# A ConvNeXt block on one core: convolution two tiles ahead and layernorm one tile ahead, both spread over the octets of the MLP

## The chip, the cores and the metric

The kernel runs on one core of a Trainium2 chip. A core has a matrix engine (PE, with its weight loads shown apart as PEld), a vector engine (DVE), a scalar engine (ACT), a general engine (POOL), and SyncE (SP), which here only issues transfers. The matrix engine writes into PSUM, a small memory of its own; everything else lies in SBUF. Each engine works through its own queue in order, and waits where a semaphore has not come yet.

The metric is the device time of one execution in microseconds, lower is better. A profile is one execution taken by the hardware profiler: it gives the start and the length of each instruction, and what its engine waited for.

## The reference

```python
def reference(x, dw, w1, b1, w2, b2, gamma):        # x: 1 x 512 x 512 x 96, bf16
    xp = jnp.pad(x, ((0,0),(pad,pad),(pad,pad),(0,0)))
    for i in range(3):
        for j in range(3):
            out = out + xp[:, i:i+H, j:j+W, :] * dw[i, j][None, None, None, :]
    h = _layernorm(out, axis=-1)
    h = jnp.einsum('bhwc,ce->bhwe', h, w1) + b1      # 96 -> 384
    h = _gelu(h)
    h = jnp.einsum('bhwe,ec->bhwc', h, w2) + b2      # 384 -> 96
    return x + gamma[None, None, None, :] * h
```

A depthwise 3x3 convolution, a layernorm over the 96 channels, an MLP with gelu, a scale by gamma, and a residual.

## The kernel before

**Tiles.** The image is cut into 20 tiles: four strips of 128 rows, each cut into five blocks of 102 or 103 columns. A tile goes through three stages.

1. *Convolution* (`conv_steps`, L156). `load_xw` (L141, transfer on L151, on SP) brings the tile's pixels into `xw`, with columns of the image on the partitions. For each channel three matmuls (L168), one for each vertical offset, multiply `xw` by a band matrix `brev` that holds the three horizontal taps. Four channels, 12 matmuls, make a "quad" in one PSUM tile `ps_conv` (two buffers). A quad is then evacuated into `zt`, three of four by DVE (L173) and every fourth by ACT (L175). A tile has 24 quads.
2. *Layernorm* (`ln_steps`, L182). For each of the 102 or 103 columns DVE takes statistics of the 96 channels (L189). The columns are worked in four parts; after the statistics of a part, POOL computes the reciprocal deviation (six small operations, then a power, L200) and multiplies `zt` by it in place (L201). The mean is not subtracted: it is folded into the weights at the start.
3. *MLP* (`mlp_octet`, L214), eight columns at a time, called an octet; a tile has 13, the last one shorter. PE transposes eight columns into `pst` (L218, one PSUM buffer), they are copied to `y` (by ACT, L221, or by DVE, L223), six matmuls make `h` (L235, two buffers), three gelus on ACT make `gt` (L239, four buffers), and for each column four matmuls make `po` (L251 and L255, one PSUM buffer for four columns). DVE adds the residual `xh` to four columns at a time (L259) and SP stores the octet (L262). The residual `xh` of an octet is loaded on SP (L211) two octets ahead, in three buffers.

**Order.** At the start two tiles are loaded, and tile 0 gets its convolution and its layernorm. Then one loop runs over all octets of all tiles (L312). While tile `ti` goes through its octets, the generator `chain` (L298) gives the work of tile `ti + 1`: in the first half of the octets (`CONV_FRAC` 0.5, six octets) its 24 quads, four to an octet; in the second half its layernorm steps. In that second half `y` is copied by ACT, else by DVE. The load of tile `ti + 2` is issued at the start of tile `ti`. `xw` has two buffers and `zt` two.

The program text sets which work is before which where both are ready. What each engine's queue holds in the end is laid out when the program is built; the trace shows it.

**Start.** The band matrix is made from a table `r_dram` by eight transfers (L100), four issued by SP and four by POOL, each 36 x 128 runs of 127 elements.

The parts that the change touches:

```python
    xw_pool = ctx.enter_context(tc.tile_pool(name="xw", bufs=2))
    zt_pool = ctx.enter_context(tc.tile_pool(name="zt", bufs=2))
    ...
            if c4 % EVAC_MOD != EVAC_MOD - 1:
                nc.vector.tensor_copy(out=zt[:, :n, 4 * c4:4 * c4 + 4], in_=ps[:, :, :n].rearrange("p s q -> p q s"))
            else:
                nc.scalar.copy(out=zt[:, :n, 4 * c4:4 * c4 + 4], in_=ps[:, :, :n].rearrange("p s q -> p q s"))
```

Of the kernel before, what the change touches and what calls it, by code (L numbers as in the profile page):

```python
# [8 lines left out]
BF16 = mybir.dt.bfloat16  # L9
F32 = mybir.dt.float32  # L10
# [3 lines left out]
P = 128  # L14
NMAX = 126
# [3 lines left out]
def _w_blocks(W):  # L19
    blocks = []  # L20
    w0 = 0
    nblk = -(-W // NMAX)
    sizes = [W // nblk + (1 if i < W % nblk else 0) for i in range(nblk)]
    for n in sizes:
        lo = max(0, w0 - 1)
        hi = min(W, w0 + n + 1)
        need = hi - lo
        kload = min(P, -(-need // 16) * 16)
        c_base = lo
        extra = kload - need  # L30
# [12 lines left out]
def kernel(  # L43
# [11 lines left out]
    nc = tc.nc  # L55
    B_, H, W, C = x.shape
# [4 lines left out]
    CA = C + 1  # L61
    NM = 3 * C
    NB = NMAX + 1
    RL = 256

    const = ctx.enter_context(tc.tile_pool(name="const", bufs=1))
    dram = ctx.enter_context(tc.tile_pool(name="dram", bufs=1, space=bass.MemoryType.DRAM))

# [3 lines left out]
        out=ident[:], in_=ident[:], pattern=[[-1, P]], compare_op=ALU.not_equal,  # L72
        fill=1.0, base=0, channel_multiplier=1,
    )

    mhalf = const.tile([P, NMAX], F32, name="mhalf")
    nc.gpsimd.memset(mhalf[:], -0.5)
    sel0 = const.tile([P, P], BF16, name="sel0")
    nc.vector.memset(sel0[:], 0.0)
# [12 lines left out]
    brev = const.tile([P, NM, NB], BF16, name="brev")  # L92
    NCH = 8
    mper = NM // NCH
    for ch in range(NCH):
        m0 = ch * mper
        src = bass.AP(tensor=r_dram.tensor, offset=r_dram.offset + m0 * RL,
                      ap=[[1, P], [RL, mper], [1, NB]])
        with nc.allow_non_contiguous_dma("hankel band expansion"):
            (nc.sync if ch % 2 == 0 else nc.gpsimd).dma_start(out=brev[:, m0:m0 + mper, :], in_=src)  # L100

    w1s = const.tile([C, E], BF16, name="w1s")
    nc.sync.dma_start(out=w1s[:], in_=w1)
# [21 lines left out]
                                       op0=ALU.mult, op1=ALU.add)  # L125

    xw_pool = ctx.enter_context(tc.tile_pool(name="xw", bufs=2))
    zt_pool = ctx.enter_context(tc.tile_pool(name="zt", bufs=2))
    st_pool = ctx.enter_context(tc.tile_pool(name="st", bufs=1))
    y_pool = ctx.enter_context(tc.tile_pool(name="y", bufs=2))  # L130
    g_pool = ctx.enter_context(tc.tile_pool(name="g", bufs=4))
# [7 lines left out]
    tiles = [(h0,) + wb for h0 in range(0, H, P) for wb in _w_blocks(W)]  # L139

    def load_xw(h0, w0, n, c_base, kload, k_off):  # L141
        xw = xw_pool.tile([P, 130, C], BF16, name="xw")
# [8 lines left out]
            nc.sync.dma_start(out=xw[:kload, s_lo:s_hi, :], in_=src)  # L151
        return xw

    EVAC_MOD = 4

    def conv_steps(xw, n, kload, k_off):  # L156
        kt = kload
        b0 = NB - k_off - n
        assert b0 >= 0
        zt = zt_pool.tile([P, NMAX, CA], BF16, name="zt")  # L160
        nc.gpsimd.memset(zt[:, :, C:CA], 1.0)
        yield zt
        for c4 in range(C // 4):
            ps = ps_conv.tile([P, 4, NMAX], F32, name="ps_conv")
            for s in range(4):
                c = 4 * c4 + s
                for i in range(3):
                    nc.tensor.matmul(  # L168
                        ps[:, s, :n], lhsT=xw[:kt, i:i + P, c], rhs=brev[:kt, c * 3 + i, b0:b0 + n],
                        start=(i == 0), stop=(i == 2),  # L170
                    )
            if c4 % EVAC_MOD != EVAC_MOD - 1:
                nc.vector.tensor_copy(out=zt[:, :n, 4 * c4:4 * c4 + 4], in_=ps[:, :, :n].rearrange("p s q -> p q s"))  # L173
            else:
                nc.scalar.copy(out=zt[:, :n, 4 * c4:4 * c4 + 4], in_=ps[:, :, :n].rearrange("p s q -> p q s"))  # L175
            yield None

    def ln_parts(n):
        npart = 4 if n > 64 else (2 if n > 16 else 1)
        return [((n * k) // npart, (n * (k + 1)) // npart) for k in range(npart)]  # L180

    def ln_steps(zt, n):  # L182
        st = st_pool.tile([P, NMAX, 6], F32, name="st")
        d = st_pool.tile([P, NMAX], F32, name="d")
        v = st_pool.tile([P, NMAX], F32, name="v")
        rstd = st_pool.tile([P, NMAX], F32, name="rstd")
        for (qa, qb) in ln_parts(n):
            for q in range(qa, qb):
                nc.vector.bn_stats(st[:, q, :], zt[:, q, 0:C])  # L189
                if (q - qa) % 16 == 15:  # L190
                    yield None
            sl = slice(qa, qb)
            me, m2e, mo, m2o = st[:, sl, 1], st[:, sl, 2], st[:, sl, 4], st[:, sl, 5]
            nc.gpsimd.tensor_tensor(out=d[:, sl], in0=me, in1=mo, op=ALU.subtract)  # L194
            nc.gpsimd.tensor_tensor(out=d[:, sl], in0=d[:, sl], in1=d[:, sl], op=ALU.mult)
            nc.gpsimd.tensor_tensor(out=v[:, sl], in0=m2e, in1=m2o, op=ALU.add)
            nc.gpsimd.tensor_scalar(out=v[:, sl], in0=v[:, sl], scalar1=1.0 / C, scalar2=LN_EPS, op0=ALU.mult, op1=ALU.add)
            nc.gpsimd.tensor_scalar(out=d[:, sl], in0=d[:, sl], scalar1=0.25, scalar2=None, op0=ALU.mult)
            nc.gpsimd.tensor_tensor(out=v[:, sl], in0=v[:, sl], in1=d[:, sl], op=ALU.add)
            nc.gpsimd.tensor_tensor(out=rstd[:, sl], in0=v[:, sl], in1=mhalf[:, sl], op=ALU.pow)  # L200
            nc.gpsimd.tensor_tensor(out=zt[:, sl, 0:C], in0=zt[:, sl, 0:C],  # L201
                                    in1=rstd[:, sl].unsqueeze(2).to_broadcast([P, qb - qa, C]), op=ALU.mult)
            yield None
# [60 lines left out]
    T = len(tiles)  # L264
    xws = {}
    zts = {}

    def start_conv(ti):
        h0, w0, n, c_base, kload, k_off = tiles[ti]
        gen = conv_steps(xws.pop(ti), n, kload, k_off)  # L270
        zts[ti] = next(gen)
        return gen

    def drain(gen):
        for _ in gen:
            pass

    for ti in range(min(2, T)):
        xws[ti] = load_xw(*tiles[ti])
    drain(start_conv(0))  # L280
    drain(ln_steps(zts[0], tiles[0][2]))

    goct = [(ti, q0, nb) for ti in range(T) for (q0, nb) in octets_of(tiles[ti][2])]
# [8 lines left out]
    for gi in range(min(PF, len(goct))):  # L292
        do_prefetch(gi)

    nextgen = None
    CONV_FRAC = 0.5

    def chain(ti1):  # L298
        for _ in start_conv(ti1):
            yield "conv"  # L300
        for _ in ln_steps(zts[ti1], tiles[ti1][2]):
            yield "ln"

    def nsteps(ti1):
        n1 = tiles[ti1][2]
        nconv = C // 4
        nln = 0
        for (qa, qb) in ln_parts(n1):
            nln += (qb - qa) // 16 + 1
        return nconv, nln  # L310

    for gi, (ti, q0, nb) in enumerate(goct):  # L312
        h0, w0, n = tiles[ti][:3]
        nocts = len(octets_of(n))
        oi = q0 // 8
        if oi == 0:
            if ti + 2 < T:
                xws[ti + 2] = load_xw(*tiles[ti + 2])
            if ti + 1 < T:
                nextgen = chain(ti + 1)  # L320
                nconv, nln = nsteps(ti + 1)
                conv_octs = max(1, int(nocts * CONV_FRAC))
                ln_octs = max(1, nocts - conv_octs)
                plan = []
                for o in range(nocts):
                    if o < conv_octs:
                        k = -(-nconv * (o + 1) // conv_octs) - (-(-nconv * o // conv_octs))
                    else:
                        oo = o - conv_octs
                        k = -(-nln * (oo + 1) // ln_octs) - (-(-nln * oo // ln_octs))  # L330
                    plan.append(k)
                if nocts == 1:
                    plan = [nconv + nln]
            else:
                nextgen = None
        if gi + PF < len(goct):
            do_prefetch(gi + PF)
        in_ln_phase = (nextgen is not None) and nocts > 1 and oi >= max(1, int(nocts * CONV_FRAC))
        mlp_octet(zts[ti], pre.pop(0), h0, w0, n, q0, nb, y_on_act=in_ln_phase)
        if nextgen is not None:  # L340
            for _ in range(plan[oi]):
                if next(nextgen, None) is None and False:
                    break
            if oi == nocts - 1:
                drain(nextgen)
                nextgen = None
        if oi == nocts - 1:
            zts.pop(ti, None)


# [28 lines left out]
```

## Time and profile before

| | |
|---|---|
| median of 4 runs | 1521.56 us |
| lowest to highest | 1520.33 to 1522.35 us |
| the profiled execution, its own time | 1522.35 us |
| its span, first to last instruction | 1520.6 us |
| mean granted clock of the matrix engine | 0.943 |

How to read the rows that follow in the prediction. A group of the page reads: line, engine, operation, output <- input with partitions x elements and type, count, then busy time in us and the mean length of one in ns, then the idle time of the engine just before them and what ended most of it. A row of windows reads: start:end, length, then for each engine busy us and (instructions), the granted clock, the mean share of the 16 transfer engines in work, and GB/s. A row of the timeline reads: start, length, engine, line, operation, tile, count of merged instructions, and in brackets the idle time before and who ended it. SPq is SP's queue, and the length there is the time that the issue of a transfer took. In the row of slices a digit is the busy share of a fortieth of the span (38 us) in tenths.

### The profile page before, as it was taken

The numbers are of one execution on the slowest core, as the hardware profiler recorded it, in microseconds if no ns is written. First come the engines' busy times: TensorE is split into PE (matmuls) and PEld (weight loads), VectorE is DVE, ScalarE is ACT, GpSimd is POOL, SyncE is SP. The second block draws the span as 40 slices with busy tenths as digits, with TensorE's granted clock in tenths as the row PEclk, the third lists the DMA queues.
The fourth block names the chain that finished last, engine by engine and source line by source line (L and its number), as shares of the span: only waits on it lengthen the run. The fifth ranks groups of instructions, "written<-read, shape, count | busy, mean of one in ns | idle before, by whom it ended". The sixth has DMA issues, their size and how long they took to land.

```text
span 1520.6 us, 42250 instructions
## 1 busy us (share of the span) xinstructions
PE 1300.1 (86%) x17562; PEld 1047.0 (69%) x17562; DVE 919.2 (60%) x3063; ACT 944.6 (62%) x1055; POOL 834.5 (55%) x681
## 2 busy tenths in 40 slices
PE   0359889898989798989898988989898989898988
PEld 0348677776868686858686767767686868586756
DVE  0176675747565656566665657574756565657654
ACT  0026666666666667575757666666666666767677
POOL 2056928374655647382929292837465564738390
PEclk9979899998989999989898999999999989999999
DMA  9964563636262727273645546363626272722223
GB/s 186 203 113 93 125 106 106 127 92 127 86 126 91 133 84 140 75 145 82 136 91 128 100 121 107 104 126 92 126 88 130 83 136 84 136 74 82 67 90 97
DMA packets 386052, 168.80 MB, mean 111 GB/s; under 512 B 318019, under 2 KB 384772, under 8 KB 385860
## 3 DMA queue, kind: packets, MB, share of 16 engines
q1 hardware_dynamic: 384708, 161.42, 49.3%
q0 software_dynamic: 1152, 4.68, 1.5%
q8 instruction: 137, 2.24, 0.7%
q14 instruction: 55, 0.45, 0.1%
HBM read 115.59 MB, written 50.48 MB: 109 GB/s over the span
## 4 chain that ended last, share of the span: by engine, by line
PE 62%; DVE 17%; ACT 12%; issue 3%; SPq 3%; DMA 3%; ACTq 0%; DVEq 0%
PE ps_conv L168 21%; PE h L235 17%; PE po L255 14%; DVE st L189 12%; ACT gt L239 9%; PE po L251 6%; PE pst L218 4%; DVE ot L259 4%; SPq L100 3%; ACT zt L175 1%; ACT y L221 1%; DMA brev<-r_dram 1%; DMA r_dram<-rs 1%; DVE y L223 1%; DMA out_dram<-ot 1%
## 5 line engine op out<-in xcount | busy, mean ns | idle before, releaser
L239 ACT ACTIVATE gt<-h 128x1024 bf16<-128x1024 f32 x760 | 730.9, 1018 | 357.2 <-PE h L235 305.1
L168 PE MATMUL ps_conv<-brev,xw 112*128 112x102 bf16 (+1 forms) x5760 | 453.8, 226 | 58.0 <-DMA brev<-r_dram 56.7
L259 DVE TENSOR_TENSOR ot<-po,xh 128x384 bf16<-128x384 f32 (+1 forms) x520 | 284.8, 548 | 355.7 <-PE po L255 350.8
L235 PE MATMUL h<-y,w1aug 97*128 97x512 bf16 (+2 forms) x1560 | 448.9, 391 | 58.9 <-ACT y L221 38.3
L255 PEld LDWEIGHTS <-gt 128*128 128x128 bf16 x6144 | 392.4, 102 | 125.0 <-issue 62.8
L168 PEld LDWEIGHTS <-xw 112*128 112x128 bf16 x5760 | 412.7, 155 | 92.6 <-issue 67.0
L255 PE MATMUL po<-w2g,gt 128*128 128x96 bf16 x6144 | 467.9, 213 | 9.8 <-ACT gt L239 9.6
L251 PE MATMUL po<-b2g,sel 128*128 128x96 bf16 x2048 | 390.9, 212 | 56.9 <-DVE ot L259 50.5
L200 POOL TENSOR_TENSOR rstd<-v,mhalf 128x25 f32<-128x25 f32 (+1 forms) x80 | 356.2, 4452 | 6.3
L173 DVE CAST zt<-ps_conv 128x408 bf16<-128x408 f32 (+1 forms) x360 | 241.6, 679 | 184.3 <-PE ps_conv L168 177.1
L201 POOL TENSOR_TENSOR zt<-zt,rstd 128x2400 bf16<-128x2400 bf16 (+1 forms) x80 | 343.6, 4295 | 6.3
L189 DVE BATCH_NORM_STATS2 st<-zt 128x6 f32<-128x96 bf16 x2048 | 334.9, 239 | 14.9 <-ACT zt L175 14.7
L235 PEld LDWEIGHTS <-w1aug 97*128 97x128 bf16 x1560 | 144.0, 102 | 157.4 <-issue 96.7
L194 POOL TENSOR_TENSOR d<-st 128x25 f32<-128x25 f32 (+1 forms) x80 | 21.2, 266 | 389.4 <-DVE st L189 389.4
L251 PEld LDWEIGHTS <-sel 128*128 128x128 bf16 x2048 | 211.7, 103 | 28.1 <-issue 9.5
L218 PE MATMUL pst<-ident,zt 128*97 128x128 bf16 x2048 | 186.0, 226 | 33.3 <-ACT y L221 19.7
L218 PEld LDWEIGHTS <-zt 128*97 128x97 bf16 x2048 | 154.9, 131 | 62.6 <-issue 28.6
L175 ACT CAST zt<-ps_conv 128x408 bf16<-128x408 f32 (+1 forms) x120 | 82.8, 690 | 174.7 <-PE ps_conv L168 174.7
L221 ACT COPY y<-pst 97x1024 bf16<-97x1024 bf16 (+2 forms) x133 | 132.3, 995 | 32.1 <-PE pst L218 32.0
L223 DVE COPY y<-pst 97x1024 bf16<-97x1024 bf16 (+1 forms) x127 | 86.8, 684 | 38.3 <-PE pst L218 22.6
L148 POOL MEMSET xw<- 112x96 bf16 x5 | 0.9, 178 | 118.9 <-PE ps_conv L168 118.9
L146 POOL MEMSET xw<- 112x96 bf16 x5 | 0.8, 176 | 81.3 <-issue 49.8
(29 smaller groups left out, 146.5 us busy)
## 6 DMA issues: line engine op xcount, KB each, us to landing
xh<-in_x_dram SPq DMA_DIRECT2D x240, 192.0 KB, 2.5
out_dram<-ot SPq DMA_DIRECT2D x240, 192.0 KB, 1.9
xw<-in_x_dram SPq DMA_DIRECT2D x10, 2730.0 KB, 16.6
xw<-in_x_dram SPq DMA_DIRECT2D x10, 2709.0 KB, 16.4
brev<-r_dram SPq DMA_DIRECT2D x4, 1143.0 KB, 14.9
brev<-r_dram POOLq DMA_DIRECT2D x4, 1143.0 KB, 17.6
xh<-in_x_dram SPq DMA_DIRECT2D x12, 144.0 KB, 2.3
out_dram<-ot SPq DMA_DIRECT2D x12, 144.0 KB, 1.8
```

The costliest lines, as they stand in the source:

```text
L168: nc.tensor.matmul(ps[:, s, :n], lhsT=xw[:kt, i:i + P, c], rhs=brev[:kt, c * 3 + i, b0:b0 + n], start=(i == 0), stop=(i == 2),)
L173: nc.vector.tensor_copy(out=zt[:, :n, 4 * c4:4 * c4 + 4], in_=ps[:, :, :n].rearrange("p s q -> p q s"))
L189: nc.vector.bn_stats(st[:, q, :], zt[:, q, 0:C])
L200: nc.gpsimd.tensor_tensor(out=rstd[:, sl], in0=v[:, sl], in1=mhalf[:, sl], op=ALU.pow)
L201: nc.gpsimd.tensor_tensor(out=zt[:, sl, 0:C], in0=zt[:, sl, 0:C], in1=rstd[:, sl].unsqueeze(2).to_broadcast([P, qb - qa, C]), op=ALU.mult)
L218: nc.tensor.transpose(pst[:CA, jj * P:(jj + 1) * P], zt[:, q0 + jj, 0:CA], ident[:])
L221: nc.scalar.copy(out=y[:CA, :nb * P], in_=pst[:CA, :nb * P])
L235: nc.tensor.matmul(h1[:, sl, :npx], lhsT=w1aug[:CA, ec * P:(ec + 1) * P], rhs=y[:CA, hf * 4 * P:hf * 4 * P + npx], start=True, stop=True)
L239: nc.scalar.activation(out=gt[:, :, :widths[0]], in_=h1[:, :, :widths[0]], func=AF.Gelu_apprx_tanh)
L251: nc.tensor.matmul(po[:, pos, :], lhsT=sel0[:], rhs=b2g[:], start=True, stop=False)
L255: nc.tensor.matmul(po[:, pos, :], lhsT=gt[:, sl, (jj % 4) * P:(jj % 4 + 1) * P], rhs=w2g[:, ec, :], start=False, stop=(ec == NE - 1))
L259: nc.vector.tensor_tensor(out=ot[:, 4 * pt:4 * pt + n4, :], in0=po[:, :n4, :], in1=xhb[:, 4 * pt:4 * pt + n4, :], op=ALU.add)
```

## The change

Seven things are changed.

1. While tile `ti` goes through its octets, the convolution of tile `ti + 2` and the layernorm of tile `ti + 1` run beside it, as two generators, each spread evenly over all 13 octets (`spread`). After each octet come about two quads, then one or two layernorm steps.
2. Before the loop, the convolutions of tiles 0 and 1 run, and the load of tile 2 is issued; then comes the layernorm of tile 0. In the loop the load of tile `ti + 3` is issued at the start of tile `ti`.
3. `zt` has three buffers instead of two. `xw` keeps two.
4. All evacuations are on DVE (`EVAC_MOD = 0`), and all `y` copies too (`Y_MOD = 0`). The code for deferred evacuations on ACT is there, but is not used.
5. A layernorm step has 8 statistics instead of 16.
6. The tiles of layernorm and convolution are sized for 103 columns (`NT`) instead of 126, and the band matrix keeps only the 112 columns that are used (`NBS`) instead of 127.
7. Of the eight band transfers, four are issued by ACT instead of SP; POOL's four stay.

```diff
+    tiles = [(h0,) + wb for h0 in range(0, H, P) for wb in _w_blocks(W)]
+    NT = max(t[2] for t in tiles)
+    B0MIN = min(NB - t[5] - t[2] for t in tiles)
+    NBS = NB - B0MIN
...
-            (nc.sync if ch % 2 == 0 else nc.gpsimd).dma_start(out=brev[:, m0:m0 + mper, :], in_=src)
+            (nc.scalar if ch % 2 == 0 else nc.gpsimd).dma_start(out=brev[:, m0:m0 + mper, :], in_=src)
...
-    zt_pool = ctx.enter_context(tc.tile_pool(name="zt", bufs=2))
+    zt_pool = ctx.enter_context(tc.tile_pool(name="zt", bufs=3))
...
-    EVAC_MOD = 4
+    EVAC_MOD = 0
+    Y_MOD = 0
...
-                if (q - qa) % 16 == 15:
+                if (q - qa) % 8 == 7:
                     yield None
...
+    def spread(nsteps, nocts):
+        return [-(-nsteps * (o + 1) // nocts) - (-(-nsteps * o // nocts)) for o in range(nocts)]
...
     for ti in range(min(2, T)):
         xws[ti] = load_xw(*tiles[ti])
     drain(start_conv(0))
+    if T > 2:
+        xws[2] = load_xw(*tiles[2])
+    if T > 1:
+        drain(start_conv(1))
     drain(ln_steps(zts[0], tiles[0][2]))
...
+            if ti + 3 < T:
+                xws[ti + 3] = load_xw(*tiles[ti + 3])
+            conv_gen = start_conv(ti + 2) if ti + 2 < T else None
+            ln_gen = ln_steps(zts[ti + 1], tiles[ti + 1][2]) if ti + 1 < T else None
+            plan_c = spread(C // 4, nocts)
+            plan_l = spread(ln_nsteps(tiles[ti + 1][2]), nocts) if ti + 1 < T else None
...
+        mlp_octet(zts[ti], pre.pop(0), h0, w0, n, q0, nb, y_on_act=(Y_MOD > 0 and oi % Y_MOD == Y_MOD - 1))
...
+        if conv_gen is not None:
+            for _ in range(plan_c[oi]):
+                r = next(conv_gen, None)
+                if callable(r):
+                    deferred.append(r)
+        if ln_gen is not None:
+            for _ in range(plan_l[oi]):
+                next(ln_gen, None)
```

More of the change, by code (lines that the diff above doesn't have):

```diff
@@ L74 @@
     )
-    mhalf = const.tile([P, NMAX], F32, name="mhalf")
+    mhalf = const.tile([P, NT], F32, name="mhalf")
     nc.gpsimd.memset(mhalf[:], -0.5)
@@ L91 @@
     nc.sync.dma_start(out=r_dram[:], in_=rs[:])
-    brev = const.tile([P, NM, NB], BF16, name="brev")
+    brev = const.tile([P, NM, NBS], BF16, name="brev")
     NCH = 8
@@ L96 @@
         m0 = ch * mper
-        src = bass.AP(tensor=r_dram.tensor, offset=r_dram.offset + m0 * RL,
-                      ap=[[1, P], [RL, mper], [1, NB]])
+        src = bass.AP(tensor=r_dram.tensor, offset=r_dram.offset + m0 * RL + B0MIN,
+                      ap=[[1, P], [RL, mper], [1, NBS]])
         with nc.allow_non_contiguous_dma("hankel band expansion"):
-            (nc.sync if ch % 2 == 0 else nc.gpsimd).dma_start(out=brev[:, m0:m0 + mper, :], in_=src)
+            (nc.scalar if ch % 2 == 0 else nc.gpsimd).dma_start(out=brev[:, m0:m0 + mper, :], in_=src)
     w1s = const.tile([C, E], BF16, name="w1s")
@@ L137 @@
     ps_o = ctx.enter_context(tc.tile_pool(name="ps_o", bufs=1, space=bass.MemoryType.PSUM))
-    tiles = [(h0,) + wb for h0 in range(0, H, P) for wb in _w_blocks(W)]
     def load_xw(h0, w0, n, c_base, kload, k_off):
@@ L152, in load_xw @@
         return xw
-    EVAC_MOD = 4
+    EVAC_MOD = 0
+    Y_MOD = 0
     def conv_steps(xw, n, kload, k_off):
         kt = kload
-        b0 = NB - k_off - n
+        b0 = NB - k_off - n - B0MIN
         assert b0 >= 0
-        zt = zt_pool.tile([P, NMAX, CA], BF16, name="zt")
+        zt = zt_pool.tile([P, NT, CA], BF16, name="zt")
         nc.gpsimd.memset(zt[:, :, C:CA], 1.0)
@@ L163, in conv_steps @@
         for c4 in range(C // 4):
-            ps = ps_conv.tile([P, 4, NMAX], F32, name="ps_conv")
+            ps = ps_conv.tile([P, 4, NT], F32, name="ps_conv")
             for s in range(4):
@@ L171, in conv_steps @@
                     )
-            if c4 % EVAC_MOD != EVAC_MOD - 1:
-                nc.vector.tensor_copy(out=zt[:, :n, 4 * c4:4 * c4 + 4], in_=ps[:, :, :n].rearrange("p s q -> p q s"))
-            else:
-                nc.scalar.copy(out=zt[:, :n, 4 * c4:4 * c4 + 4], in_=ps[:, :, :n].rearrange("p s q -> p q s"))
-            yield None
+            dst = zt[:, :n, 4 * c4:4 * c4 + 4]
+            src = ps[:, :, :n].rearrange("p s q -> p q s")
+            if EVAC_MOD == 0 or c4 % EVAC_MOD != EVAC_MOD - 1:
+                nc.vector.tensor_copy(out=dst, in_=src)
+                yield None
+            else:
+                yield (lambda dst=dst, src=src: nc.scalar.copy(out=dst, in_=src))
     def ln_parts(n):
@@ L182, in ln_steps @@
     def ln_steps(zt, n):
[L183 to L186, printed above, removed]
+        st = st_pool.tile([P, NT, 6], F32, name="st")
+        d = st_pool.tile([P, NT], F32, name="d")
+        v = st_pool.tile([P, NT], F32, name="v")
+        rstd = st_pool.tile([P, NT], F32, name="rstd")
         for (qa, qb) in ln_parts(n):
@@ L274, in drain, with ln_nsteps @@
     def drain(gen):
-        for _ in gen:
-            pass
+        for r in gen:
+            if callable(r):
+                r()
+    def spread(nsteps, nocts):
+        return [-(-nsteps * (o + 1) // nocts) - (-(-nsteps * o // nocts)) for o in range(nocts)]
+    def ln_nsteps(n1):
+        return sum((qb - qa) // 8 + 1 for (qa, qb) in ln_parts(n1))
     for ti in range(min(2, T)):
@@ L293 @@
         do_prefetch(gi)
[L295 to L310, printed above, removed]
+    conv_gen = ln_gen = None
+    plan_c = plan_l = None
+    deferred = []
     for gi, (ti, q0, nb) in enumerate(goct):
@@ L316 @@
         if oi == 0:
[L317 to L335, printed above, removed]
+            if ti + 3 < T:
+                xws[ti + 3] = load_xw(*tiles[ti + 3])
@@ L336 @@
+            conv_gen = start_conv(ti + 2) if ti + 2 < T else None
+            ln_gen = ln_steps(zts[ti + 1], tiles[ti + 1][2]) if ti + 1 < T else None
+            plan_c = spread(C // 4, nocts)
+            plan_l = spread(ln_nsteps(tiles[ti + 1][2]), nocts) if ti + 1 < T else None
         if gi + PF < len(goct):
             do_prefetch(gi + PF)
-        in_ln_phase = (nextgen is not None) and nocts > 1 and oi >= max(1, int(nocts * CONV_FRAC))
-        mlp_octet(zts[ti], pre.pop(0), h0, w0, n, q0, nb, y_on_act=in_ln_phase)
@@ L340 @@
[L340 to L346, printed above, removed]
-        if oi == nocts - 1:
+        mlp_octet(zts[ti], pre.pop(0), h0, w0, n, q0, nb, y_on_act=(Y_MOD > 0 and oi % Y_MOD == Y_MOD - 1))
+        for fn in deferred:
+            fn()
+        deferred = []
+        if conv_gen is not None:
+            for _ in range(plan_c[oi]):
+                r = next(conv_gen, None)
+                if callable(r):
+                    deferred.append(r)
@@ L348 @@
+        if ln_gen is not None:
+            for _ in range(plan_l[oi]):
+                next(ln_gen, None)
+        if oi == nocts - 1:
+            for fn in deferred:
+                fn()
+            deferred = []
+            if conv_gen is not None:
+                drain(conv_gen)
+            if ln_gen is not None:
+                drain(ln_gen)
             zts.pop(ti, None)
```

## The prediction

> **What bounds the kernel now.** I read the page first, then the chain of waits, the windows by stage, and the timelines of DVE, SP and ACT in one tile. First the groups of the page: line, engine, operation, tile, count, then busy time and mean ns, then idle time before.
>
> ```profile
> PE 1300.1 (86%) x17562; PEld 1047.0 (69%) x17562; DVE 919.2 (60%) x3063; ACT 944.6 (62%) x1055; POOL 834.5 (55%) x681
> L239 ACT ACTIVATE gt<-h 128x1024 bf16<-128x1024 f32 x760 | 730.9, 1018 | 357.2 <-PE h L235 305.1
> L259 DVE TENSOR_TENSOR ot<-po,xh 128x384 bf16<-128x384 f32 (+1 forms) x520 | 284.8, 548 | 355.7 <-PE po L255 350.8
> L200 POOL TENSOR_TENSOR rstd<-v,mhalf 128x25 f32<-128x25 f32 (+1 forms) x80 | 356.2, 4452 | 6.3
> L173 DVE CAST zt<-ps_conv 128x408 bf16<-128x408 f32 (+1 forms) x360 | 241.6, 679 | 184.3 <-PE ps_conv L168 177.1
> L201 POOL TENSOR_TENSOR zt<-zt,rstd 128x2400 bf16<-128x2400 bf16 (+1 forms) x80 | 343.6, 4295 | 6.3
> L189 DVE BATCH_NORM_STATS2 st<-zt 128x6 f32<-128x96 bf16 x2048 | 334.9, 239 | 14.9 <-ACT zt L175 14.7
> L221 ACT COPY y<-pst 97x1024 bf16<-97x1024 bf16 (+2 forms) x133 | 132.3, 995 | 32.1 <-PE pst L218 32.0
> L223 DVE COPY y<-pst 97x1024 bf16<-97x1024 bf16 (+1 forms) x127 | 86.8, 684 | 38.3 <-PE pst L218 22.6
> ```
>
> PE is busy 86%, but that is a mean over two unlike stages. The chain of waits dates the same piece of layernorm in each tile, and the windows (PE, PEld, DVE, ACT, POOL busy with counts, then granted clock, DMA share, GB/s) split one tile:
>
> ```profile
> 219.73 1.12 DVE st L189 x7
> ...
> 581.41 8.68 DVE st L189 x55
> ...
> 1301.65 1.12 DVE st L189 x7
> ```
>
> ```profile
> 538.00:574.00 36.00, 35.93 (x540) 31.04 (x539) 20.76 (x35) 21.24 (x24) 10.80 (x9) 1.00 0.24 73
> 574.00:610.00 36.00, 28.61 (x351) 21.25 (x349) 24.94 (x119) 26.21 (x29) 30.24 (x25) 0.91 0.78 149
> 1437.00:1465.00 28.00, 21.07 (x258) 14.37 (x258) 21.25 (x110) 22.12 (x25) 23.05 (x23) 1.00 0.28 85
> ```
>
> The rows 219.73 and 1301.65 are 15 tiles apart: a tile takes 72.13 us. In its first 36 us (convolution of the next tile beside the MLP) PE never rests: 540 matmuls at 66.5 ns. In the second 36 us (layernorm of the next tile beside the MLP) PE does 351 matmuls, and the convolution, which could fill it, is used up. What holds it there stands in the queues of SP and DVE:
>
> ```profile
> 573.13 0.33 SPq L151 DMA_DIRECT2D xw<-in_x_dram  x1
> 575.13 13.03 SPq L262 DMA_DIRECT2D out_dram<-ot  x1
> 588.25 1.37 SPq L211 DMA_DIRECT2D xh<-in_x_dram  x1
> ```
>
> ```profile
> 581.33 10.62 DVE L189 BATCH_NORM_STATS2 st<-zt 128x6 f32<-128x96 bf16 x66
> 591.87 0.54 DVE L259 TENSOR_TENSOR ot<-po,xh 128x384 bf16<-128x384 f32 x1
> ```
>
> ```profile
> xw<-in_x_dram SPq DMA_DIRECT2D x10, 2709.0 KB, 16.4
> ```
>
> ```profile
> 592.00:594.00 2.00, 1.44 (x16) 1.30 (x16) 0.47 (x2) 0.22 (x1) 2.00 (x1) 0.50 0.30 88
> ```
>
> The load of a coming tile (16.4 us) starts as the convolution ends and frees its buffer. The store behind it on SP takes 13.03 us to issue, and the next residual load starts at 588.25. No octet can finish without residual and store, so the 66 statistics in a row on DVE are partly filling for a transfer. PE then restarts at a granted clock of 0.50 (last column but two). The last tile but one has no such load: its stage takes 28 us instead of 36. So of each tile's layernorm stage **8 us belong to the transfer**. In the 28 us that are left DVE sets the pace:
>
> ```profile
> 1446.01 0.56 DVE L259 TENSOR_TENSOR ot<-po,xh 128x384 bf16<-128x384 f32 x1
> 1446.48 1.21 DVE L189 BATCH_NORM_STATS2 st<-zt 128x6 f32<-128x96 bf16 x7
> ...
> 1448.06 2.64 DVE L189 BATCH_NORM_STATS2 st<-zt 128x6 f32<-128x96 bf16 x16
> 1450.75 0.56 DVE L259 TENSOR_TENSOR ot<-po,xh 128x384 bf16<-128x384 f32 x1
> ```
>
> An octet takes 4.74 us (1446.01 to 1450.75), with 7 + 16 = 23 statistics in it and DVE without a gap, though the text issues 8 to 9 an octet on average: the queue's order is not that of the text, ready work is drawn forward.
>
> **The change, part by part.**
>
> *Software pipeline.* No matmul is removed or added. PE has 17560/20 = 878 per tile; at the 66.5 ns of the convolution stage that is 58.4 us, the floor of a tile if convolution is always there to fill. So at most 13.7 us per tile is to be had.
>
> *What moves to DVE.* All y copies (L221's 133, from 995 ns on ACT to about 684 on DVE) and all evacuations of the convolution (120 from ACT, 679 each). Statistics cost less than their 239 ns, since they overlap:
>
> ```profile
> 86.52 16.53 DVE L189 BATCH_NORM_STATS2 st<-zt 128x6 f32<-128x96 bf16 x103 [0.76 <-ACT zt L175]
> ```
>
> 103 in 16.53 us, 160 ns each. DVE per tile then: 24 casts x 0.679 = 16.3, 26 residual adds x 0.548 = 14.2, 13 y x 0.684 = 8.9, 103 statistics x 0.160 = 16.5: **55.9 us**. ACT falls to 38 gelus x 1.018 = 38.7. POOL keeps 4 x (4.45 + 4.30 + six small operations, about 1.6) = 41 us, spread over the tile. So two engines, PE 58.4 and DVE 55.9, are now nearly full, and each waits for the other several times per octet through single buffers (transposes, MLP output).
>
> How much is lost to waits between two full engines no row shows. From one side it is nothing: in the convolution stage PE ran at 99.8% with DVE at 58%. From the other side stands the 28 us row, where DVE had no gap and PE had 21.07 of 28 (75%); at that rate a tile takes 78 us. In the new tile convolution always fills PE, so I stay near the first row: 94%, **62 us**.
>
> *The load.* It still comes once per tile on SP, and the code gives it no other queue. It starts when a convolution ends, which now should be near the end of a tile, so that the next convolution (24 x 12 matmuls x 66.5 ns = 19 us of PE) stands ready to fill the wait. But where waits pull convolution ahead of its plan, it ends early, and the next load meets octets without filler, as now. Bounds 0 and 8 us; I take 3. So **65 us** per tile.
>
> *Start.* Before, the order is:
>
> ```profile
> 20.13 51.23 SPq L100 DMA_DIRECT2D brev<-r_dram  x4
> ...
> 63.17 5.39 PE L168 MATMUL ps_conv<-brev,xw 112*128 112x103 bf16 x60 [56.29 <-DMA brev<-r_dram]
> ...
> 101.12 1.09 PE L218 MATMUL pst<-ident,zt 128*97 128x128 bf16 x8 [13.65 <-POOL zt L201]
> ...
> 104.74 1.94 ACT L239 ACTIVATE gt<-h 128x1024 bf16<-128x1024 f32 x2 [16.96 <-PE h L235]
> ```
>
> ```profile
> DMA  9964563636262727273645546363626272722223
> 63.00:87.00 24.00, 22.17 (x308) 21.32 (x309) 13.25 (x21) 4.79 (x7) 0.18 (x1) 1.00 1.00 160
> ```
>
> The four band loads moved from SP to ACT hold ACT's queue, which has nothing to do before 104.74; if that cover went, gelu would wait for their issue. The narrower band has the same number of runs. The DMA engines are 9 tenths busy in the first two slices (76 us), so I count 0, between -10 (15 of 127 columns fewer, and no tile load ahead in the same queue) and +5. The Trainium skill ("DMA: Bandwidth & Descriptors", section "Issuing engines are not separate DMA queues") says the same against this part: another issuing engine saves only its own issue time. The second tile's convolution, 24 quads at DVE's 0.7, stands ahead of layernorm 0: about 11 us until its statistics find room, from the first transposes at 101 to 112. Part of the third convolution can run in that wait: -6. Bounds: 0 (statistics slip in between) and 20 (a whole convolution).
>
> *End.* Two tiles now run without convolution. The pace of such octets with y on DVE is that of the last tile:
>
> ```profile
> 1473.23 3.06 ACT L239 ACTIVATE gt<-h 128x1024 bf16<-128x1024 f32 x3 [0.63 <-PE h L235]
> ...
> 1506.68 3.06 ACT L239 ACTIVATE gt<-h 128x1024 bf16<-128x1024 f32 x3 [0.66 <-PE h L235]
> ```
>
> 3.72 us per octet (nine in 33.45), x 12.8 (2048 transposes / 20 tiles / 8) = 48. Last tile 48 + 3 for the final store; the one before it 48 + 6, since its statistics, drawn forward 23 to an octet, make DVE 5.3 us long in four octets.
>
> **Sum:** 112 - 6 + 17 x 65 + 62 (the last window with convolution has no load) + 54 + 51 = 1378 of span. The profiled execution took 1522.35 for a span of 1520.6, 1.75 more, and lies 0.8 above the median 1521.56: I say **1380 us**. With P for a tile, the time is 210 + 18 P.
>
> **Rivals.**
>
> *PE-bound.* Order and load cost next to nothing, P = 60 to 61: 1290 to 1308. For it: 99.8% in the convolution stage. Against it: DVE at 93% of P.
>
> *The load keeps its price.* Convolution is pulled ahead in each wait, ends early, and the load again meets octets without filler: P = 62 + 8 = 70, 1470. For it: the load left at 573.13, half a tile before the text asks for it, the moment that its buffer was free. Nothing in the change holds it back.
>
> *Slower: y behind statistics.* In the text, the next octet's y copy now stands behind two casts and eight statistics on DVE. If the queue follows the text, PE waits after its transposes (8 matmuls, 0.5 us) for a cast 0.68, statistics 1.28 and y 0.68, about 2.1 us an octet net, 12.8 x 2.1 = 27 us a tile: P = 62 + 27, near 90, 1830. It decides where P passes 72.9, that is from 0.6 us an octet on top of the forecast's 65 (7.9/12.8). Against it: statistics are drawn forward, so few should be left to stand ahead of y.
>
> *DVE works one after the other.* If operations did not overlap, the statistics would cost their 239 ns, DVE 64 us a tile, and with the same slip and load P = 64/0.94 + 3 = 71, 1490. Against it: 160 ns from start to start. The Trainium skill ("VectorE: DVE Perf Modes", section "The DRAIN you can't avoid") states this as the rule, the next operation waiting until the pipeline of the one before is empty, with an exception for what the page calls not held; the row of 103 speaks against the rule here.
>
> *It doesn't do what it says.* The queue order pulls everything forward, convolution ends at half a tile as now, and P stays at 71 to 73: 1488 to 1524.
>
> **Chances.** Forecast (P 62 to 68, 1326 to 1434) 0.52; PE-bound 0.14; load 0.22; y behind statistics 0.08; DVE without overlap 0.02; no effect 0.02. About 0.2% is what a measurement of this kernel can tell from no change. Faster 0.90, same 0.02, slower 0.08. The range 1295 to 1480 leaves out the lower edge of the second case, the upper edge of the third, and what lies above 1480.
>
> **What would show it.** Right: the chain's repeat falls from 72 to about 65; no slice of layernorm without convolution on PE; granted clock near 1.00 where 0.50 stood; DVE above 80%, ACT below 60%. The load step is wrong if the windows after each L151 issue still show PE at half; the slip step if PE waits for DVE's y or ot by more than 3 us a tile; the floor if matmuls take over 66.5 ns with PE full. A y wait above 1 us an octet would turn the sign.

## The result and the profile after

The changed kernel takes **1372.59 us** (median of 8 runs, 1371.83 to 1374.75) against 1521.39 us before on the same chips (13 runs): a ratio of 0.9026, 95% interval 0.9017 to 0.9035. The profiled execution has a span of 1369.9 us, where 1378 was forecast.

The page of the changed kernel, the same groups as before (line numbers have moved by six or so: L265 is the residual add, L179 the evacuation, L195 the statistics, L229 the y copy):

```profile
PE 1240.8 (91%) x17562; PEld 1014.5 (74%) x17562; DVE 1042.9 (76%) x3316; ACT 748.0 (55%) x801; POOL 834.5 (61%) x681
L265 DVE TENSOR_TENSOR ot<-po,xh 128x384 bf16<-128x384 f32 (+1 forms) x520 | 281.8, 542 | 166.7 <-PE po L261 165.4
L179 DVE CAST zt<-ps_conv 128x408 bf16<-128x408 f32 (+1 forms) x480 | 323.3, 682 | 93.2 <-PE ps_conv L172 85.6
L195 DVE BATCH_NORM_STATS2 st<-zt 128x6 f32<-128x96 bf16 x2048 | 362.7, 242 | 19.5 <-POOL v L202 17.9
L229 DVE COPY y<-pst 97x1024 bf16<-97x1024 bf16 (+1 forms) x260 | 174.9, 673 | 39.1 <-PE pst L224 37.7
```

PE does the same 17562 matmuls; its busy time fell from 1300 to 1241 us, in the main with the clock: the mean granted clock rose from 0.943 to 0.976, which by itself would give 1300 x 0.943 / 0.976 = 1256, by estimate. DVE took over the copies, ACT went from 62% to 55%.

The timeline of DVE dates the ends of tiles: an octet of seven columns is a tile's last, and its second residual add has three columns (288 elements). These two are 16 tiles apart:

```profile
198.78 0.44 DVE L265 TENSOR_TENSOR ot<-po,xh 128x288 bf16<-128x288 f32 x1
...
1209.66 0.44 DVE L265 TENSOR_TENSOR ot<-po,xh 128x288 bf16<-128x288 f32 x1
```

A tile takes 63.18 us on the mean (1010.88/16), instead of 72.13. But it isn't one figure: ten of the sixteen take 60 to 62 us, six take 64.1 to 68.0. One of each kind in the windows (stretch, its length, busy time of PE, PEld, DVE, ACT and POOL, granted clock, DMA share, GB/s), and the queue of SP in each:

```profile
577.71:639.39 61.68, 60.88 (x877) 49.87 (x876) 51.44 (x166) 37.44 (x40) 41.13 (x33) 1.00 0.65 129
448.00:515.78 67.78, 63.69 (x894) 52.46 (x892) 52.61 (x167) 37.84 (x42) 41.41 (x33) 0.95 0.58 118
```

```profile
577.71 0.40 SPq L154 DMA_DIRECT2D xw<-in_x_dram  x1
582.77 12.35 SPq L268 DMA_DIRECT2D out_dram<-ot  x1
```

```profile
448.00 0.33 SPq L154 DMA_DIRECT2D xw<-in_x_dram  x1
448.38 16.39 SPq L268 DMA_DIRECT2D out_dram<-ot  x1
```

In the ordinary tile PE is busy 60.88 of 61.68 us at a granted clock of 1.00, although SP's queue still stands for 12.35 us behind the load: the convolution of the tile after next fills that time. In the long tile the load stands one store and one residual load earlier in the queue, and SP stands for 16.39 us. DVE then has no residual add between these two:

```profile
450.31 0.54 DVE L265 TENSOR_TENSOR ot<-po,xh 128x384 bf16<-128x384 f32 x1
...
470.78 0.54 DVE L265 TENSOR_TENSOR ot<-po,xh 128x384 bf16<-128x384 f32 x1
```

That is 20.5 us; in the ordinary tile the same gap is 15.0 us (585.37 to 600.40). In its second half, from 461 on, PE has nothing but convolution. That does not run out: of the 288 convolution matmuls of this window (windows of L172) 200 run by 472, and some 90 are left. But its evacuations share DVE's queue with the statistics of the next tile, and `ps_conv` has two buffers. A row of PE, two of DVE, and a window behind them:

```profile
466.87 2.83 PE L172 MATMUL ps_conv<-brev,xw 112*128 112x102 bf16 x36 [2.19 <-DVE zt L179]
```

```profile
463.61 2.64 DVE L195 BATCH_NORM_STATS2 st<-zt 128x6 f32<-128x96 bf16 x16
466.17 1.21 DVE L179 CAST zt<-ps_conv 128x408 bf16<-128x408 f32 x2
```

```profile
469.00:472.00 3.00, 2.31 (x29) 2.19 (x27) 3.00 (x13) 0.00 (x0) 2.84 (x3) 0.50 0.00 0
```

PE waits 2.19 us for an evacuation that stands behind 16 statistics, and after that its granted clock is 0.50 in this window; over the tile the mean is 0.95. All six long tiles have such waits. They are nearly all of this row of the kernel's waits (total, times, longest):

```profile
PE ps_conv L172 <- DVE zt L179: 14.1, 14, 2.2
```

The start is longer than forecast. The timeline of all engines, DVE and PE rows:

```profile
105.06 12.69 DVE L195 BATCH_NORM_STATS2 st<-zt 128x6 f32<-128x96 bf16 x79
...
117.67 0.67 DVE L229 COPY y<-pst 97x1024 bf16<-97x1024 bf16 x1
118.27 1.42 DVE L179 CAST zt<-ps_conv 128x408 bf16<-128x408 f32 x2
...
137.55 2.65 DVE L195 BATCH_NORM_STATS2 st<-zt 128x6 f32<-128x96 bf16 x16 [17.86 <-POOL v L202]
...
140.84 1.86 PE L241 MATMUL h<-y,w1aug 97*128 97x512 bf16 x4 [17.40 <-DVE y L229]
```

DVE stands still for 17.86 us, in front of statistics that wait for POOL. They are statistics of tile 1, drawn forward ahead of the second octet's y copy; there is one buffer for the statistics of a whole tile, and POOL still reads those of tile 0 from it. PE waits 17.40 us for the y behind them.

### The profile page after: what moved, and what is told of

Read it like the earlier page. It is cut to its first block, busy times and chain, and to the rows that moved or that the text cites. A ratio compares the mean times of both kernels' runs of the same rounds, so it can differ in the third digit from the quotient of the medians.

```text
span 1369.9 us, 42194 instructions
## 1 busy us (share of the span) xinstructions
PE 1240.8 (91%) x17562; PEld 1014.5 (74%) x17562; DVE 1042.9 (76%) x3316; ACT 748.0 (55%) x801; POOL 834.5 (61%) x681
## 4 chain that ended last, share of the span: by engine, by line
PE 68%; ACT 11%; DVE 10%; DMA 5%; issue 3%; POOL 2%; ACTq 0%; SPq 0%; DVEq 0%
PE h L241 22%; PE ps_conv L172 19%; PE po L261 16%; ACT gt L245 11%; PE po L257 6%; PE pst L224 5%; DVE zt L179 4%; DVE st L195 4%; DMA brev<-r_dram 3%; DVE y L229 2%; DMA r_dram<-rs 1%; POOL rstd L206 1%; DVE ot L265 1%; POOL zt L207 1%; DMA b2b<-in_b_dram 0%
## 5 line engine op out<-in xcount | busy, mean ns | idle before, releaser
L172 PE MATMUL ps_conv<-brev,xw 112*128 112x102 bf16 (+1 forms) x5760 | 451.3, 228 | 71.3 <-DMA brev<-r_dram 54.9
L172 PEld LDWEIGHTS <-xw 112*128 112x128 bf16 x5760 | 415.8, 155 | 100.5 <-issue 69.4
L241 PE MATMUL h<-y,w1aug 97*128 97x512 bf16 (+2 forms) x1560 | 430.9, 376 | 33.5 <-DVE y L229 18.4
L261 PE MATMUL po<-w2g,gt 128*128 128x96 bf16 x6144 | 436.8, 207 | 0.4 <-ACT gt L245 0.2
L265 DVE TENSOR_TENSOR ot<-po,xh 128x384 bf16<-128x384 f32 (+1 forms) x520 | 281.8, 542 | 166.7 <-PE po L261 165.4
L261 PEld LDWEIGHTS <-gt 128*128 128x128 bf16 x6144 | 367.2, 98 | 51.1 <-issue 7.4
L179 DVE CAST zt<-ps_conv 128x408 bf16<-128x408 f32 (+1 forms) x480 | 323.3, 682 | 93.2 <-PE ps_conv L172 85.6
L257 PE MATMUL po<-b2g,sel 128*128 128x96 bf16 x2048 | 374.7, 207 | 9.0 <-DVE b2g L125 5.8
L195 DVE BATCH_NORM_STATS2 st<-zt 128x6 f32<-128x96 bf16 x2048 | 362.7, 242 | 19.5 <-POOL v L202 17.9
L257 PEld LDWEIGHTS <-sel 128*128 128x128 bf16 x2048 | 204.0, 100 | 29.4 <-DVE sel L85 1.5
L229 DVE COPY y<-pst 97x1024 bf16<-97x1024 bf16 (+1 forms) x260 | 174.9, 673 | 39.1 <-PE pst L224 37.7
L165 POOL MEMSET zt<- 128x103 bf16 x20 | 12.1, 648 | 149.2 <-PE pst L224 149.2
L204 POOL TENSOR_SCALAR d<-d 128x25 f32<-128x25 f32 (+1 forms) x80 | 24.1, 302 | 6.3
```

The costliest lines, as they stand in the source:

```text
L172: nc.tensor.matmul(ps[:, s, :n], lhsT=xw[:kt, i:i + P, c], rhs=brev[:kt, c * 3 + i, b0:b0 + n], start=(i == 0), stop=(i == 2),)
L179: nc.vector.tensor_copy(out=dst, in_=src)
L229: nc.vector.tensor_copy(out=y[:CA, :nb * P], in_=pst[:CA, :nb * P])
L241: nc.tensor.matmul(h1[:, sl, :npx], lhsT=w1aug[:CA, ec * P:(ec + 1) * P], rhs=y[:CA, hf * 4 * P:hf * 4 * P + npx], start=True, stop=True)
L257: nc.tensor.matmul(po[:, pos, :], lhsT=sel0[:], rhs=b2g[:], start=True, stop=False)
L261: nc.tensor.matmul(po[:, pos, :], lhsT=gt[:, sl, (jj % 4) * P:(jj % 4 + 1) * P], rhs=w2g[:, ec, :], start=False, stop=(ec == NE - 1))
```

## The experiments

**Theory.** A tile is bound by PE as long as convolution is at hand in every octet; it also covers the load. What is lost beyond that is the start (the statistics buffer) and the six long tiles (load and queue order). An expectation of experiment 2 has it that the convolution runs out in the long tiles; the rows above show that it is held up by its evacuations. **Rivals.** The moves from ACT to DVE make the gain; the depth alone makes it; DVE, not PE, is the bound now. All ratios are to the kernel before on the same chip.

| kernel | us | ratio (95%) |
|---|---|---|
| changed kernel | 1372.59 | 0.9026 (0.9017 to 0.9035) |
| two statistics buffers | 1354.68 | 0.8902 (0.8889 to 0.8915) |
| changed, load issued by ACT | 1460.61 | 0.9598 (0.9584 to 0.9613) |
| before, load issued by ACT | 1691.41 | 1.1116 (1.1099 to 1.1132) |
| before, all copies on DVE | 1560.54 | 1.0247 (1.0220 to 1.0275) |
| before, load in ten pieces | 1476.11 | 0.9696 (0.9680 to 0.9713) |
| changed, not interleaved | 1571.68 | 1.0322 (1.0306 to 1.0339) |
| changed, copies shared with ACT | 1393.02 | 0.9150 (0.9136 to 0.9164) |
| two statistics buffers, load in ten pieces | 1323.92 | 0.8697 (0.8682 to 0.8713) |
| the same without bias matmuls | 1247.75 | 0.8199 (0.8179 to 0.8219) |
| the same, layernorm 0 first | 1327.70 | 0.8725 (0.8705 to 0.8744) |
| changed, band transfers on SP | 1373.26 | 0.9024 (0.9006 to 0.9042) |

**1. Two statistics buffers.**

```diff
-    st_pool = ctx.enter_context(tc.tile_pool(name="st", bufs=1))
+    st_pool = ctx.enter_context(tc.tile_pool(name="st", bufs=2))
```

> The changed kernel with two buffers for the statistics tiles instead of one; the order of every queue stays. Theory (the start is lengthened because the statistics of tile 1 stand on DVE ahead of the first octets and wait 17.9 us for POOL to free the only statistics buffer): that wait goes, the tiles after it stay at about 62 us, so 1353 to 1358 us, 15 to 19 less than the changed kernel. Rival (POOL's layernorm of tile 0, 10.6 us for each quarter, paces the first octets anyway): 1368 to 1373.

1354.68 us, 17.9 less. The timeline of its DVE:

```profile
105.62 12.69 DVE L195 BATCH_NORM_STATS2 st<-zt 128x6 f32<-128x96 bf16 x79
118.23 0.67 DVE L229 COPY y<-pst 97x1024 bf16<-97x1024 bf16 x1
118.82 1.42 DVE L179 CAST zt<-ps_conv 128x408 bf16<-128x408 f32 x2
120.11 2.64 DVE L195 BATCH_NORM_STATS2 st<-zt 128x6 f32<-128x96 bf16 x16
```

The same 16 statistics now run at 120.11, with no wait. The order of the instructions on every engine is that of the changed kernel, so this is the wait by itself.

**2. The load issued by ACT**, in the changed kernel and in the one before.

```diff
-            nc.sync.dma_start(out=xw[:kload, s_lo:s_hi, :], in_=src)
+            nc.scalar.dma_start(out=xw[:kload, s_lo:s_hi, :], in_=src)
```

> The changed kernel with the tile load issued by ACT instead of SP, so that stores and residual loads no longer stand behind it in one queue. Theory (six of the tiles take 64 to 68 us instead of 61.7 because the queue of SP stands still for 12 to 16 us and the convolution runs out): all tiles near 61.5, about 26 us less, 1343 to 1352 us. Rival (the longer tiles come from DVE's order, the transfer is only beside it): within 5 us of 1372.

> The kernel before with the tile load issued by ACT instead of SP. Theory (8 us of each layernorm stage belong to the transfer's place in SP's queue, 16 tiles): 16 x 8 = 128 us less, 1380 to 1410 us. Rival (the layernorm stage is held by DVE and ACT, or the transfers share the same engines whichever queue they are in): 1500 us or more.

The theory missed twice, in the other direction: 1460.61 and 1691.41 us. The second lies where its rival put it, at 1500 or more, but far beyond the kernel before, which neither expected. The load no longer stands ahead of anything in SP's queue. These are the issues of the second kernel from 635 to 640 us, a load, a store and a residual load under it, with the median time to landing in the last column; and then its timeline of SP and of DVE:

```profile
xw<-in_x_dram ACTq DMA_DIRECT2D x1, 2730.0 KB, 18.0
out_dram<-ot SPq DMA_DIRECT2D x1, 192.0 KB, 6.4
xh<-in_x_dram SPq DMA_DIRECT2D x1, 192.0 KB, 7.1
```

```profile
637.81 0.52 SPq L211 DMA_DIRECT2D xh<-in_x_dram  x1
```

```profile
637.26 15.73 DVE L189 BATCH_NORM_STATS2 st<-zt 128x6 f32<-128x96 bf16 x98
652.91 0.54 DVE L259 TENSOR_TENSOR ot<-po,xh 128x384 bf16<-128x384 f32 x1
```

The residual left at 637.81 and had landed by 645. But DVE's queue was laid out anew: 98 statistics in a row, not 66, now stand ahead of the next residual add, which starts at 652.91, right behind them and 8 us after the landing. So the order on DVE costs by itself. The first kernel shows the same. It has no residual add between these two, 22.4 us, although SP issued the residual load at 307.58 and stood free, and PE waits for evacuations five times as long as in the changed kernel:

```profile
306.58 0.54 DVE L265 TENSOR_TENSOR ot<-po,xh 128x384 bf16<-128x384 f32 x1
...
329.01 0.56 DVE L265 TENSOR_TENSOR ot<-po,xh 128x384 bf16<-128x384 f32 x1
```

```profile
PE ps_conv L172 <- DVE zt L179: 70.8, 78, 2.1
```

This pair does not tell what the transfer costs alone.

**3. The load in ten pieces, each held behind the store of an octet.** This takes the standstill of SP away and with it the reason for the order.

```diff
-                xws[ti + 3] = load_xw(*tiles[ti + 3])
+                load_gen = load_steps(ti + 3)      # tile and memsets; then 13 rows a step
...
+        if load_gen is not None:
+            with tc.issue_after(store.ins):
+                next(load_gen, None)
```

In the kernel before it is the same with tile `ti + 2`.

> The kernel before with the tile load cut into ten pieces of 13 rows, one issued by SP behind the store of each octet, in place of one load in one go. Theory (the layernorm stage is 36 us instead of 28 because SP's queue stands still behind the load, and because the queue of DVE is laid out around that with 66 statistics in a row): 16 tiles at 28 us, 128 us less, 1385 to 1405 us. Rival (the stage is held by ACT's y copies and DVE alone, the load lies beside them): 1500 us or more.

> The changed kernel with both: two statistics buffers, and the tile load in ten pieces behind the stores. Theory (the six tiles of 64 to 68 us come to 61.5, the start gains 17.9): 1355 - 25, 1325 to 1338 us. Rival (convolution used to cover the load, so cutting it up gains nothing, and 300 more issues on SP cost): 1350 us or more.

The second did a little better than expected: 1323.92 us, 30.8 less than with two statistics buffers alone. Its 16 tiles take 60.5 to 62.1 us, all of them, and the waits of PE for evacuations (14.1 us in the changed kernel) no longer stand in the list of its waits. The first missed: 1476.11 us, 46 less than before, where 128 were expected. Two rows of its chain of waits, 16 tiles apart, and two of DVE's timeline, one octet apart:

```profile
283.00 4.16 DVE st L189 x26
...
1390.35 4.16 DVE st L189 x26
```

```profile
568.23 0.56 DVE L259 TENSOR_TENSOR ot<-po,xh 128x384 bf16<-128x384 f32 x1
...
572.97 0.56 DVE L259 TENSOR_TENSOR ot<-po,xh 128x384 bf16<-128x384 f32 x1
```

A tile takes 69.2 us instead of 72.13: the load with its order cost 2.9 us a tile there, not 8. Without it the layernorm stage goes at 4.74 us an octet. DVE, without a gap between statistics and adds, sets that pace at first; it stays about the same when the statistics are done, and what holds it then was not traced. With the load in place the octets after the standstill went faster, 3.5 us each on the mean (from the add at 591.87 to the one at 609.39, five octets), with the statistics already done: the time was made good in part. That this is the reason is read from the rows, not tested.

**4. The move to DVE alone**, in the kernel before.

```diff
-            if c4 % EVAC_MOD != EVAC_MOD - 1:
+            if True:
...
-        mlp_octet(zts[ti], pre.pop(0), h0, w0, n, q0, nb, y_on_act=in_ln_phase)
+        mlp_octet(zts[ti], pre.pop(0), h0, w0, n, q0, nb, y_on_act=False)
```

> The kernel before with all evacuations and all y copies on DVE, without the deeper pipeline. Theory (the gain is the convolution that fills PE, the move to DVE by itself gains nothing): within 2% of before, 1500 to 1550 us. Rival (ACT's slower copies were what held the layernorm stage, the move makes most of the gain): 1450 us or less.

1560.54 us, 2.5% slower than before, a little beyond the theory's range. The move makes none of the gain; without the pipeline it costs.

**5. The same depth, not interleaved.**

```diff
-            plan_c = spread(C // 4, nocts)
-            plan_l = spread(ln_nsteps(tiles[ti + 1][2]), nocts) if ti + 1 < T else None
+            half = max(1, nocts // 2)
+            plan_c = spread(C // 4, half) + [0] * (nocts - half)
+            plan_l = [0] * half + spread(ln_nsteps(tiles[ti + 1][2]), nocts - half) if ti + 1 < T else None
```

> The changed kernel with the same depth (convolution two tiles ahead, layernorm one ahead) but not interleaved: the 24 quads in the first six octets, the layernorm steps in the last seven. Theory (what pays is that convolution is at hand on PE in every octet, and that the load of a tile falls where convolution is left): the second half has no filler again, 70 to 72 us a tile, 1470 to 1515 us. Rival (the depth alone pays, since no stage waits for the one before it any more): within 15 us of 1372.

1571.68 us, 199 more than the changed kernel, slower than the kernel before, and beyond the theory's range. The chain of waits dates a tile, and DVE's timeline shows the block:

```profile
416.83 5.33 DVE st L195 x34
...
491.80 5.32 DVE st L195 x34
```

```profile
640.05 7.43 DVE L195 BATCH_NORM_STATS2 st<-zt 128x6 f32<-128x96 bf16 x46
647.41 0.54 DVE L265 TENSOR_TENSOR ot<-po,xh 128x384 bf16<-128x384 f32 x1
```

75 us a tile. The load left at 625.62 (SP's timeline), as the convolution ended: from 635 to 648 PE has no convolution matmul and is busy 3.87 of 13 us. The depth only makes the interleaving possible; by itself it gains nothing.

**6. Copies shared with ACT**, `EVAC_MOD = 4` and `Y_MOD = 2` in the changed kernel.

> The changed kernel with every fourth evacuation and every second y copy on ACT again (DVE 55.9 - 6 x 0.68 - 6 x 0.68 = 47.7 us a tile, ACT 38.7 + 10.1 = 48.8). Theory (PE is the bound at 98% of a tile, DVE has room enough): 1360 to 1385 us. Rival (DVE at about 90% is what keeps a tile at 61.7 to 68 instead of 58.4): 1345 us or less.

1393.02 us, 1.4% slower than the changed kernel by the ratios and outside both ranges. Most tiles take about 64 us. DVE has less to do (66% busy) and nothing gets faster, so DVE's load was not the bound. Why it gets slower was not followed up.

**7. Less work for PE**, in the kernel with two statistics buffers and the load in pieces.

```diff
-            nc.tensor.matmul(po[:, pos, :], lhsT=sel0[:], rhs=b2g[:], start=True, stop=False)
...
-                               rhs=w2g[:, ec, :], start=False, stop=(ec == NE - 1))
+                               rhs=w2g[:, ec, :], start=(ec == 0), stop=(ec == NE - 1))
```

> The kernel with two statistics buffers and the load in pieces, without the 2048 bias matmuls (L257; the output then lacks b2 times gamma). They come 42 ns apart, 87 us of PE in all, and take nothing from DVE. Theory (with convolution always at hand PE is the bound of a tile): 1235 to 1265 us. Rival (DVE at 79% and the waits between the engines are the bound): 1300 us or more.

This kernel leaves out the bias b2. 1247.75 us: the ratio falls by 0.0498, 76 us, for 87 us of matmuls taken away. The page with and without them:

```profile
PE 1229.6 (93%) x17562; PEld 1007.6 (76%) x17562; DVE 1049.9 (79%) x3316; ACT 740.6 (56%) x801; POOL 834.6 (63%) x681
PE 1138.8 (91%) x15514; PEld 921.9 (74%) x15514; DVE 1035.3 (83%) x3316; ACT 738.0 (59%) x801; POOL 834.4 (67%) x681
```

The other engines have the same number of instructions and nearly the same busy time, and the time falls with PE's. In this kernel PE is the bound.

**8. Layernorm 0 first**, in the same kernel: the two lines before the loop exchanged.

> The same kernel, with the layernorm of tile 0 ahead of the convolution of tile 1 in the text before the loop. Theory (the first transposes at 115 us instead of 101 come from statistics of tile 0 that stand behind the evacuations of tile 1): the first transposes 8 to 12 us earlier, 1311 to 1317 us. Rival (the convolution of tile 1 then only stands ahead of the first octet's residual adds instead): 1320 to 1328 us.

1327.70 us; the intervals overlap, no gain. The rival was right. DVE's timeline:

```profile
102.38 0.67 DVE L229 COPY y<-pst 97x1024 bf16<-97x1024 bf16 x1
...
121.98 0.54 DVE L265 TENSOR_TENSOR ot<-po,xh 128x384 bf16<-128x384 f32 x1
```

The first y comes 14.3 us earlier (116.66 before), but 22 evacuations of tile 1 stand between it and the first residual add, which comes only 1.1 us earlier (123.05 before).

**9. The band on SP again.**

```diff
-            (nc.scalar if ch % 2 == 0 else nc.gpsimd).dma_start(out=brev[:, m0:m0 + mper, :], in_=src)
+            (nc.sync if ch % 2 == 0 else nc.gpsimd).dma_start(out=brev[:, m0:m0 + mper, :], in_=src)
```

> The changed kernel with the four band transfers issued by SP again instead of ACT. Theory (the transfers share the same 16 engines, which are full in the first 76 us, and ACT has nothing else to do): within 5 us of 1372.6. Rival (SP's queue is free earlier, so that the band or the tiles land sooner): 1380 us or more.

1373.26 us, the same. That part of the change is worth nothing.

## Why the prediction was right, and where it was not

The time came out 7 us under the forecast, and the cause was the forecast one. That it came so close is luck: the first tile was put 28 us too short and the next sixteen 29 us too long. In spans: 1378 forecast, 1369.9 measured.

- **The bound.** Right. With convolution at hand PE is full (60.88 of 61.68 us), and run 7 shows, in the improved kernel, that PE's work sets the time. Run 5 shows that it is the filler in each octet that pays.
- **The tile, 65 us.** Measured 63.18, over the 16 tiles 29 us less. The parts were off more. The floor of 58.4 was too low: it took the mean of the convolution stage, 66.5 ns a matmul, for all 878, but that stage holds 36 of the wide matmuls of `h` (512 columns) in 540, the ordinary tile 80 in 877, and these take 272 ns of PE each (21.75 us for the 80). Ordinary tiles measure 877 matmuls in 60.88 us, 69.4 ns each. In return there is almost no slip between PE and DVE in an ordinary tile (0.8 us without work on PE), where 3.6 us were put. In the whole execution PE waited for a y three times (the waits of the changed kernel: total, times, longest):

```profile
PE h L241 <- DVE y L229: 18.4, 3, 17.4
```

  and 17.4 of 18.4 us are the one wait of the start.
- **DVE, 55.9 us a tile and above 80%.** Too high: 51.4 us and 76%. The casts, adds and copies were counted at their full length, but they overlap as the statistics do: the copy at 118.23 in experiment 1 lasts 0.67 us, and the cast behind it starts after 0.59.
- **The load, 3 us a tile.** Ordinary tiles pay nothing, as the forecast had it: convolution fills the wait. Six tiles pay 2.6 to 6.4 us above 61.5, 27 us in all: 1.7 a tile. The size was about right, but not the reason, for convolution had not ended early in them; PE waited for its evacuations behind statistics, about 14 of the 27 us, and then ran in part at the lower clock. Run 3 takes 30.8 us away. Run 2 shows that such an order costs without any standstill of SP; what the standstill costs alone was not separated, as the pieces remove both.
- **"8 us belong to the transfer."** Wrong as a reading of the kernel before. Two stages of different make-up were subtracted. Run 3 gives 2.9 us a tile for load and order together. It did no harm to the forecast, which took 3 of it between bounds of 0 and 8, with no row for the 3.
- **The start, 112 - 6.** This step failed. The first transposes came at 115.8, near the 112; but the end of the first tile came at 198.78, where 112 - 6 + 65 = 171 was the forecast. 17.9 of the 28 us are the wait for the only statistics buffer, shown by run 1. Of the other 10, 3.8 are the later transposes; the rest was not traced. Statistics drawn forward were expected, that they would run into a buffer was not. The further gain sought there, layernorm 0 first, is not to be had (run 8).
- **The end, 54 + 51.** 47.8 and 47.3 us for the last two tiles (timeline of DVE), and 4.6 from the last tile's short octet to the end: 5 us too much, because DVE's statistics did not hold up the last tile but one.
- **The band, 0.** Right (run 9: 1373.26 against 1372.59 us). The Trainium skill ("DMA: Bandwidth & Descriptors", section "Issuing engines are not separate DMA queues"), by which another issuing engine saves only its own issue time, agrees with this run.
- **Rivals.** y behind statistics fell: a wait of 18.4 us in all, not 27 a tile. DVE one after the other fell: DVE is busy 51.44 us a tile, not 64. The load that keeps its price came partly true, in six tiles, but not by its mechanism. PE-bound was right for the ordinary tiles (61.5 us) and wrong for the time, since the start and the six tiles cost more.

The version with two statistics buffers and the load in pieces, 1323.92 us, beats both kernels: 13% below the kernel before, and 3.6% below the changed one by the ratios (0.8697 against 0.9026).

## What to carry to other kernels

Work that one engine can do at any time is worth most when it is spread so that some of it is left wherever another engine or a queue stands still; running further ahead without spreading made this kernel slower. When work is drawn forward across tiles, each single-buffered tile that it writes is a place where a whole in-order queue can stop, so look for such a wait at the start, where there is no slack yet. Filler helps only as long as its own outlet is open: here convolution was left in the long tiles, but its evacuations stood behind statistics on DVE. And moving a large transfer to another queue also moves the order that is laid out around it: cutting it into pieces, each held behind a known instruction, changed both in the wanted direction.

## What was not expected of the hardware

With the tile load on ACT's queue, a store on SP during it issued in 0.34 us, and the residual load behind it landed in 7.1 us, in the window shown in experiment 2. With all on one queue the store behind the load took 12 to 17 us to issue, and the residual load behind that had not left yet. So the large load does slow small transfers on another queue (the median landing of a residual load is 2.5 us), but the greater part of their delay, here, came from its standing ahead of them in their own. The kernels with the load on ACT's queue were slower all the same (experiment 2).

The load itself took little longer: 17.2 us in that kernel, 16.4 in the one before.

```profile
xw<-in_x_dram ACTq DMA_DIRECT2D x10, 2709.0 KB, 17.2
```
